# Windowed attention with a feed-forward layer: values of two pairs of heads in one block amid a first layer's products, with a new opening order and a last step that ends by token block

## Chip, cores and metric

The kernel runs on one core of one Trainium2 chip. The metric is the device time of one execution in microseconds (us): the median of 3 runs before is 913.11 us (913.05 to 916.48).

## The reference, cut to what matters

```python
B, H, S, D = 8, 8, 576, 64                     # q and k are multiplied by 8 when drawn
scores = (1 / np.sqrt(D)) * q @ k^T
mask_plain = (rel >= 0) & (rel < 32)           # heads 0 to 3; rel = query - key
mask_dil = (rel >= 0) & (rel < 128) & (rel % 4 == 0)    # heads 4 to 7
attn = softmax(where(mask, scores, -1e9))
x = (attn @ v).transpose(0, 2, 1, 3).reshape(4608, 512)
h = x @ w_in                                   # 512 x 2048
g = where(h >= 1, h, where(h <= -1, 0, (h + 1)**2 / 4))
return g @ w_out                               # 2048 x 512
```

(Shortened; the weights arrive as 64-bit floats.)

## The kernel before

**Attention.** The 64 heads are numbered n = 8 b + h and go in pairs (n even). Queries lie in six tiles of 96, each with its 128 keys. Heads 0 to 15 use plain fp32 matmuls and are part of the opening; for heads from 16 on (`native`), q and k are cast to a high part (`qs`, `kk` on ScalarE, L238 and L241) and a low part (`q_low` on VectorE, L245; `k_low` on GpSimd, L249). Scores come in pairs of tiles: `score_block(m, 0)`, `(m, 2)`, `(m, 4)`, two matmuls each (L332, bank `s`). VectorE masks (L356) and reduces (`lowest`, L284), ScalarE takes the exponential with its sum (`exp`, L382), GpSimd normalises (L419), VectorE transposes 32x32 blocks into `pt` (L430), and TensorE multiplies by the values (`weighted`, L532, bank `o`). The result is x, already transposed, cut in two: `x_high` copies into `xh` on ScalarE (L568), `x_low` subtracts into `xl` on VectorE (L573).

**Feed-forward.** The 4608 tokens are 9 blocks of 512 (`TOK`), each with 16 slices of 128 of the hidden dimension: 144 steps. `layer1(s, c)` for c = 0 to 3 makes 12 matmuls of 512 columns into one `h` bank (L598). Then a chain on two engines: `clamped` (VectorE, `y`, L608), `squared` (ScalarE, L611), `activated` (VectorE, into `h`, L614), `g_high` (ScalarE, `gh`, L621), `g_low` (VectorE, `gl`, L625), the last reader of the bank. `gh` and `gl` have two buffers each. `layer2(s - 2, m)` for m = 0 to 3 makes 12 matmuls from `gh` and `gl` into four `acc` banks (L637), two steps behind. The eight PSUM banks are two for `h`, two for `att` (scores, values), four for `acc`.

**What sets the order.** Steps up to 17 follow `OPENING`, a list of tokens written out by hand for all five engines: `S2.1` is the score of head 2, tile 1, `r` a reduction, `e` an exponential, `T` a transposition on TensorE with its copy `p`, `V` a value block with `x` and `l` behind it, `A` and `B` the two layers, `wi0` a load of weights, `W5` five spins. From step 18 on, TensorE's and SyncE's order is the program's, and ScalarE, VectorE and GpSimd get theirs from the scheduler. The loop at the end of the program runs layer 1 of step s, slot 2s, layer 2 of step s - 2, slot 2s + 1; `place(u, ...)` puts scores, transpositions and `values` of a pair into numbered slots, u = 27 + 4 (n - 16) onwards:

```python
place(u + 8, lambda n=n: transpose(n + 1))
place(u + 11, lambda n=n: values(n))
```

So a pair's two value blocks (`o{n}_0`, `o{n}_1`) stand together between a first layer and a second.

Of the kernel before, what the change touches and what calls it, by code (L numbers as in the profile page):

```python
# [31 lines left out]
DM, DF = 512, 2048  # L32
# [13 lines left out]
msk k0 q0 Q0 K0 q2 k2 q4 k4 S0.0 q6 S1.0 S0.1 S1.1 wi0 r0.0 r1.1 e0.0 k6 r1.0 r0.1 S0.2 e1.0 S1.2 v4 S0.3 S1.3  # L46
S0.4 e0.1 S1.4 S0.5 wi1 S1.5 e1.1 r0.2 r0.3 e0.2 r1.3 r1.5 k8 e0.3 r1.2 W2 S2.0 S3.0 r1.4 S2.1 e1.3 S3.1 r0.4
S2.2 S3.2 r0.5 e1.5 S2.3 v6 S3.3 S2.4 e1.2 r2.2 S3.4 S2.5 r3.2 S3.5 e1.4 r2.0 r2.3 wo1 e0.4 r3.0 r3.1 e0.5
r3.3 wo0 r3.4 e3.0 r2.1 i0 e3.3 r2.4 W5 S4.0 S5.0 r2.5 S4.1 e3.4 S5.1 i1 R0 S4.2 z2 R1 S5.2 r3.5 e3.1 S4.3 v0
S5.3 r4.1 e3.2 r5.0 r5.2 e3.5 v2 r4.3 S6.0 S7.0 awi0 r5.1 S6.1 n0 S7.1 r4.2 S6.2 S7.2 i3 r4.0 S6.3 e2 S7.3 k10  # L50
R3 r5.3 r7.3 r7.1 e5.1 r7.2 n3 e5.0 T0.0 r7.0 r6.3 e4.1 S4.4 wi2 S5.4 r6.1 S4.5 e4.0 S5.5 r6.0 r6.2 e4.2 u2
wi9 S6.4 n1 S7.4 e6.1 S6.5 S7.5 e6.3 r5.4 wi4 i2 e6.0 r6.4 R2 r4.4 e6.2 n2 r6.5 e4.3 p0.0 e6.5 q8 r5.5 r4.5
e6.4 r7.5 W8 T3.0 r7.4 e4.5 T1.0 i6 e4.4 R6 p3.0 T1.1 wi3 n6 T2.0 bwi0 p1.1 T3.1 i4 T0.1 p1.0 p2.0 wi6 e5.3
p3.1 V0.0 p0.1 R4 jwi0 e5.5 T6.0 e5.4 wo2 e7.1 n4 T6.1 hwi0 V0.1 x0.0.0 q10 e5.2 l0.0.0 awi1 T4.0 u5 T2.1
x0.1.0 V2.0 e7.5 e7.2 lwi0 p6.1 e7.3 p4.0 e7.4 x0.1.1 i5 l0.1.0 e7.0 p6.0 R5 u7 A0.0 n5 p2.1 x2.0.0 awi2
l0.1.1 T4.1 i7 l2.0.0 V2.1 awo0 R7 n7 T5.0 bwi1 T5.1 x2.1.0 wi14 p5.0 p4.1 T7.0 x2.1.1 wo4 bwo0 T7.1 p5.1 V4.0
l2.1.1 wi7 l2.1.0 bwi2 S8.0 wi5 jwi1 S9.0 S8.1 x4.0.1 x4.0.0 S9.1 V4.1 wi11 l4.0.1 p7.0 hwi1 v8 A0.1 l4.0.0
# [750 lines left out]
```

## Time and profile before

| what | us |
|---|---|
| median of 3 runs | 913.11 |
| lowest and highest | 913.05, 916.48 |
| profiled execution, own time | 912.37 |
| its span | 910.6 |
| TensorE busy | 898.5 (99%) |
| VectorE, ScalarE, GpSimd busy | 671.5, 492.8, 231.4 |

The span is shorter than the execution's own time by 1.8 us that lie outside of it. Busy time counts matmuls whose starts follow one another closely; their ends are modelled, so the distance between two starts is the better measure of what a matmul takes. A wait of an engine is listed with the operation that ended it.

### The profile page before, as it was taken

The numbers are of one execution on the slowest core, as the hardware profiler recorded it, in microseconds if no ns is written. First come the engines' busy times: TensorE is split into PE (matmuls) and PEld (weight loads), VectorE is DVE, ScalarE is ACT, GpSimd is POOL, SyncE is SP. The second block draws the span as 40 slices with busy tenths as digits, with TensorE's granted clock in tenths as the row PEclk, the third lists the DMA queues.
The fourth block names the chain that finished last, engine by engine and source line by source line (L and its number), as shares of the span: only waits on it lengthen the run. The fifth ranks groups of instructions, "written<-read, shape, count | busy, mean of one in ns | idle before, by whom it ended". The sixth has DMA issues, their size and how long they took to land.

```text
span 910.6 us, 14400 instructions
## 1 busy us (share of the span) xinstructions
PE 898.5 (99%) x4844; PEld 735.6 (81%) x4844; DVE 671.5 (74%) x1973; ACT 492.8 (54%) x1394; POOL 231.4 (25%) x155
## 2 busy tenths in 40 slices
PE   7999999999999999999999999999999999999998
PEld 6677887888888888888888888888888888888886
DVE  6988888888887888888888888888888643334333
ACT  7899966555555555556655555555555422223222
POOL 4546642322323222333222232322233000000000
PEclk9999999999999999999999999999999999999999
DMA  9953113122322123222312232212321010001001
GB/s 345 404 228 132 54 42 111 44 62 71 118 72 72 56 60 118 72 72 72 95 56 65 72 112 78 71 54 63 118 72 45 1 47 1 1 1 46 1 1 47
DMA packets 31178, 73.92 MB, mean 81 GB/s; under 512 B 3456, under 2 KB 4352, under 8 KB 31104
## 3 DMA queue, kind: packets, MB, share of 16 engines
q1 hardware_dynamic: 30816, 72.63, 24.4%
q8 instruction: 38, 0.62, 0.3%
q10 hardware_dynamic: 288, 0.38, 0.1%
q14 instruction: 36, 0.29, 0.1%
HBM read 63.55 MB, written 9.44 MB: 80 GB/s over the span
## 4 chain that ended last, share of the span: by engine, by line
PE 92%; ACT 3%; DMA 2%; DVE 2%; issue 0%; SPq 0%; ACTq 0%; DVEq 0%
PE acc L637 43%; PE h L598 41%; PE s L332 4%; PE o L532 3%; ACT c_place L382 1%; DMA kr<-k_in 1%; DMA wo_raw<-w_in 1%; PE s L317 1%; ACT c L382 0%; ACT xh L568 0%; ACT wi_raw L204 0%; DVE c L284 0%; PE t L462 0%; ACT wi_m L198 0%; DVE xl L573 0%
## 5 line engine op out<-in xcount | busy, mean ns | idle before, releaser
L637 PE MATMUL acc<-wo,gh 128*128 128x512 f32 x1152 | 384.0, 393 | 0.0
L598 PE MATMUL h<-xh,wi 128*128 128x512 f32 x1152 | 356.9, 391 | 0.2 <-DVE gl L625 0.2
L637 PEld LDWEIGHTS acc<-wo,gh 128*128 128x128 f32 x1152 | 216.5, 188 | 47.3
L598 PEld LDWEIGHTS h<-xh,wi 128*128 128x128 f32 x1152 | 209.3, 188 | 38.8 <-issue 0.4
L637 PE MATMUL acc<-wo,gl 128*128 128x512 f32 x576 | 225.2, 391 | 0.0
L598 PE MATMUL h<-xl,wi 128*128 128x512 f32 x576 | 224.4, 390 | 0.4 <-DVE xl L573 0.4
L249 POOL TENSOR_TENSOR kk<-kr,kk 128x608 fp32r<-128x608 f32 x48 | 93.6, 1949 | 404.7 <-ACT kk L241 395.4
L382 ACT ACTIVATE c<-c 96x128 f32<-96x128 f32 x330 | 128.9, 392 | 116.4 <-DVE c L284 116.1
L611 ACT ACTIVATE y<-y,consts 128x512 f32<-128x512 f32 x144 | 104.1, 723 | 123.4 <-DVE y L608 123.1
L621 ACT CAST gh<-h 128x512 fp32r<-128x512 f32 x144 | 84.3, 586 | 117.3 <-PE acc L637 115.8
L608 DVE TENSOR_SCALAR y<-h 128x512 f32<-128x512 f32 x144 | 99.2, 689 | 59.2 <-PE h L598 58.8
L614 DVE TENSOR_TENSOR h<-h,y 128x512 f32<-128x512 f32 x144 | 100.5, 698 | 49.2 <-ACT y L611 47.9
L598 PEld LDWEIGHTS h<-xl,wi 128*128 128x128 f32 x576 | 108.1, 188 | 24.0 <-DVE xl L573 0.9
L625 DVE TENSOR_TENSOR gl<-h,gh 128x512 fp32r<-128x512 f32 x144 | 98.7, 685 | 38.3 <-ACT gh L621 38.2
L637 PEld LDWEIGHTS acc<-wo,gl 128*128 128x128 f32 x576 | 108.1, 188 | 19.5
L430 DVE STREAM_TRANSPOSE pt<-c 32x192 f32<-32x192 f32 x288 | 106.0, 368 | 6.5 <-POOL c L419 3.1
L356 DVE TENSOR_TENSOR c<-s,fixed 96x256 f32<-96x256 f32 (+1 forms) x168 | 61.3, 377 | 34.8 <-PE s L332 33.8
L419 POOL TENSOR_TENSOR c<-c 96x768 f32<-96x768 f32 x52 | 76.3, 1467 | 24.1 <-DVE c L414 21.7
L284 DVE CUSTOM_DVE_ANT_0 c<-s,c 96x128 f32<-96x128 f32 x288 | 70.4, 280 | 1.0
L382 ACT ACTIVATION_READ_ACCUMULATOR c<-c 96x1 f32 x324 | 60.7, 187 | 0.0
L332 PEld LDWEIGHTS s<-kk,qs 128*96 128x96 f32 x288 | 46.2, 161 | 15.3
L332 PE MATMUL s<-kk,qs 128*96 128x256 f32 x288 | 57.3, 283 | 0.0
(80 smaller groups left out, 615.3 us busy)
## 6 DMA issues: line engine op xcount, KB each, us to landing
kr<-k_in SPq DMA_DIRECT2D x52, 304.0 KB, 3.3
qr<-q_in SPq DMA_DIRECT2D x52, 288.0 KB, 2.8
vt<-v_in SPq DMA_DIRECT2D x29, 384.0 KB, 4.0
out<-out SPq DMA_DIRECT2D x35, 256.0 KB, 2.5
wi_raw<-w_in SPq DMA_DIRECT2D x16, 512.0 KB, 7.7
wo_raw<-w_in SPq DMA_DIRECT2D x16, 512.0 KB, 8.8
v_place<-v_in SPq DMA_DIRECT2D x3, 384.0 KB, 7.5
k_place<-k_in SPq DMA_DIRECT2D x3, 304.0 KB, 5.8
```

The source lines that it names most:

```text
L249: nc.gpsimd.tensor_tensor(out=kk[:, 1], in0=kr, in1=kk[:, 0].bitcast(F32), op=ALU.subtract)
L332: PE.matmul(out=split_view(n, t0)[:, t - t0], lhsT=hd["qs"][:, t * QT : (t + 1) * QT], rhs=hd["ks"][:, :, t * QT : t * QT + 128], start=Tr ...
L382: nc.scalar.activation(out=c[:, t], in_=c[:, t], func=AF.Exp, bias=st[:, 0, t : t + 1], scale=-1.0, **total)
L419: engine.tensor_tensor(out=c, in0=c, in1=spread(factor(n)), op=ALU.mult)
L430: nc.vector.transpose(out=pts[n % 2][r : r + 32, :, 32 * g : 32 * g + 32], in_=heads[n]["c"][32 * g : 32 * g + 32, :, r : r + 32],)
L598: PE.matmul(out=hps[s], lhsT=ready[f"wi{f}"][:, w, 128 * c : 128 * c + 128], rhs=x[:, c], start=c == 0 and i == 0, stop=c == NC - 1 and i ...
L608: nc.vector.tensor_scalar(out=y, in0=hps[s], scalar1=-1.0, scalar2=1.0, op0=ALU.max, op1=ALU.min)
L611: nc.scalar.activation(out=ys[s], in_=ys[s], func=AF.Square, bias=half_t, scale=0.5)
L614: nc.vector.tensor_tensor(out=hps[s], in0=hps[s], in1=ys.pop(s), op=ALU.max)
L621: nc.scalar.copy(out=gs[s][0], in_=hps[s])
L625: nc.vector.tensor_tensor(out=gl, in0=hps.pop(s), in1=gh.bitcast(F32), op=ALU.subtract)
L637: PE.matmul(out=acc[m], lhsT=g[:, r], rhs=w[:, part], start=f == 0 and i == 0, stop=f == NF - 1 and i == 2,)
```

## The change

- `values` takes two pairs. For every second pair (n = 18, 22, ... 62) one block of 24 program matmuls stands after two of the four chunks of `layer1(s)`. Its first bank is the `h` bank of the step before, `h{(s + 1) % 2}`, and holds tiles 4 and 5 of the pair n; two `att` banks of 480 columns hold the rest. Of each bank all `xh` copies come first, then all `xl` subtractions.
- Half of the pairs' scores (n % 4 == 0) stand half a step later, some within a layer. Slots are counted in quarter steps.
- A second pair of `pt` buffers lies in `thirds`, the three buffers of 128 x 512 that the conversion of weights used, cleared by GpSimd at step 18. `xh`, `xl`, `h` have a tag per buffer; output rows are gathered in a former `xl` tile.
- `OPENING` is written anew; the masks come in two transfers, the first scores take three tiles instead of two, 18 instead of 13 weight tiles are cast on GpSimd (`cast_by_pool`), 6 instead of 8 heads are normalised on VectorE (`by_vector`), 16 instead of 21 copies of transposed blocks are VectorE's (`kept_by_vector`).
- The last two second layers go by token block. The last block's sum of step 142 is copied to SBUF by ScalarE, its last three products are made as two sets of 256 columns in `att` banks, added by VectorE and stored on two queues.

```diff
-OPENING = "... S6.3 e2 S7.3 k10 R3 r5.3 ... W8 T3.0 r7.4 e4.5 T1.0 i6 ..."
+OPENING = "... T1.0 v2 r4.4 e5.2 p3.0 T1.1 ... q8 W2 T3.1 e5.0 p0.1 T2.0 ..."
...
+    thirds = pool.tile([128, 3 * DM], U32, tag="m", name="thirds")
+    late_pts = thirds.bitcast(F32)[:, : 2 * NQ * QT].rearrange("p (n t j) -> p n t j", n=2, t=NQ)
...
-    first_tiles = 2
+    first_tiles = 3
...
-    def values(n):
-        for part in range(2):
-            weighted(n, part)
+    def values(n, s):
+        free = f"h{(s + 1) % 2}"
+        plan = (
+            (free, 1, ((n + 2, 4, 6),)),
+            ("att", 2, ((n, 0, 5),)),
+            ("att", 2, ((n + 2, 0, 4), (n, 5, 6))),
+        )
+        for tag, bufs, parts in plan:
+            op = ps.tile([128, 512], F32, tag=tag, name=f"o{n}_{parts[0][0]}_{parts[0][1]}", bufs=bufs)
...
             with tc.high_priority(offset=60):
-                for piece in range(len(pieces(n, part))):
-                    x_high(n, part, piece)
-                    x_low(n, part, piece)
+                lows = []
+                for pair, base, (lo, w, count, t, place) in pieces:
...
+                    nc.scalar.copy(out=xh, in_=src)
+                    lows.append((xl, src, xh))
+                for xl, src, xh in lows:
+                    nc.vector.tensor_tensor(out=xl, in0=src, in1=xh.bitcast(F32), op=ALU.subtract)
...
+    def last_block(o, gh, gl, w, rows):
+        nc.scalar.copy(out=o, in_=partial[0])
+        for i, queue in enumerate((nc.scalar, nc.sync)):
+            cols = slice(DM // 2 * i, DM // 2 * (i + 1))
+            rest = ps.tile([128, DM], F32, tag="att", name=f"rest{i}", bufs=2)[:, : DM // 2]
+            for k, (g, part) in enumerate(((gh, 0), (gl, 0), (gh, 1))):
+                PE.matmul(out=rest, lhsT=g, rhs=w[:, part, cols], start=k == 0, stop=k == 2)
+            nc.vector.tensor_tensor(out=o[:, cols], in0=rest, in1=o[:, cols], op=ALU.add)
+            queue.dma_start(out=rows[:, cols], in_=o[:, cols])
...
-        for j, at in ((0, u), (1, u + 4)):
-            place(at, lambda m=n + j: score_block(m, 0))
-            place(at + 1, lambda m=n + j: score_block(m, 2))
-            place(at + 2, lambda m=n + j: (score_block(m, 4), after(m)))
+        around = n % 4 == 0 and n > native
+        for j, ats in enumerate(((0, 0.75, 1.5), (4.5, 5.25, 6)) if around else ((0, 1, 2), (4, 5, 6))):
+            for t0, at in zip((0, 2, 4), ats):
+                place(u + at, lambda m=n + j, t0=t0: (score_block(m, t0), after(m) if t0 == 4 else None))
...
-        place(u + 11, lambda n=n: values(n))
+        if n % 4:
+            place(u + 10.5, lambda n=n, s=(u + 11) // 2: values(n - 2, s))
...
+    ends = {last + 1: [(last - 1, 0), (last - 1, 1)]}
+    ends[last + 2] = [(last, 0), (last - 1, 3), (last, 1), (last - 1, 2), (last, 2), (last, 3)]
```

How the values move, on TensorE. Before, the block of pair 32 stands between the first layer of step 51 and the second of step 49 (`h3_3` is token block 3, slice 3; `acc3_0` is block 3's first `acc`):

```order
L598 MATMUL h3_3_3906<-xh3_1957,wi3_642 128x512 x2
L598 MATMUL h3_3_3906<-xl3_1958,wi3_642 128x512
L532 MATMUL o32_0_3927<-pt0_66,vt32_3714 64x96
...
L532 MATMUL o32_1_3940<-pt0_66,vt32_3714 64x96
...
L637 MATMUL acc3_0_3865<-wo1_694,gh49_3797 128x512
L637 MATMUL acc3_0_3865<-wo1_694,gl49_3798 128x512
```

After, pairs 32 and 34 share one block, after six of the twelve matmuls of step 55 (`h3_7`). Its first rows, of the bank `o32_34_4`, are pair 34's tiles 4 and 5:

```order
L668 MATMUL h3_7_4098<-xh3_2126,wi7_988 128x512 x2
L668 MATMUL h3_7_4098<-xl3_2127,wi7_988 128x512
L628 MATMUL o32_34_4_4105<-thirds_68,vt34_3921 64x96 x4
L628 MATMUL o32_32_0_4114<-pt0_66,vt32_3679 64x96
...
L628 MATMUL o32_34_0_4129<-thirds_68,vt34_3921 64x96 x8
L628 MATMUL o32_34_0_4129<-pt0_66,vt32_3679 64x96
...
L668 MATMUL h3_7_4098<-xh3_2126,wi7_988 128x512 x2
L668 MATMUL h3_7_4098<-xl3_2127,wi7_988 128x512
...
L724 MATMUL acc3_0_3834<-wo5_1024,gh53_4004 128x512
```

The twelve pairs of matmuls of pair 32 left the place ahead of `acc`; the new block has `h` on both sides. A `x2` or `x8` counts equal rows in a run.

On ScalarE, the piece from one `y` to the next head's casts. Before, in step 58 (`y58`, `gh58`):

```order
L382 ACTIVATE c38_4323<-c38_4323 96x128 x2
L611 ACTIVATE y58_4343<-y58_4343,consts_65 128x512
L382 ACTIVATE c38_4323<-c38_4323 96x128 x2
L621 CAST gh58_4347<-h3_10_4330 128x512
L238 CAST qs39_4376<-qr39_4271 128x576
L241 CAST kk39_4377<-kr39_4273 128x608
```

After, in step 54, whose `gl` is the last reader of the bank that `o32_34_4` takes:

```order
L386 ACTIVATE c36_4026<-c36_4026 96x128 x3
L681 ACTIVATE y54_4053<-y54_4053,consts_65 128x512
L386 ACTIVATE c36_4026<-c36_4026 96x128
L242 CAST qs37_4073<-qr37_3974 128x576
L245 CAST kk37_4074<-kr37_3976 128x608
L691 CAST gh54_4057<-h3_6_4033 128x512
L386 ACTIVATE c36_4026<-c36_4026 96x128 x2
```

`gh` stood ahead of the casts `qs` and `kk`; it now stands behind them.

On VectorE, the same two pieces. Before, in step 58 (`s38_2` and `s38_4` are banks with scores of head 38, L356 masks, `ISA` is `lowest`):

```order
L608 TENSOR_SCALAR y58_4343<-h3_10_4330 128x512
L356 TENSOR_TENSOR c38_4323<-s38_2_4351,fixed_64 96x128 x2
L284 ISA c38_4323<-s38_2_4351,c38_4323 96x128
...
L614 TENSOR_TENSOR h3_10_4330<-h3_10_4330,y58_4343 128x512
L356 TENSOR_TENSOR c38_4323<-s38_4_4370,fixed_64 96x256
L625 TENSOR_TENSOR gl58_4348<-h3_10_4330,gh58_4347 128x512
L284 ISA c38_4323<-s38_4_4370,c38_4323 96x128
...
L245 TENSOR_TENSOR qs39_4376<-qr39_4271,qs39_4376 64x576
```

After, in step 54:

```order
L360 TENSOR_TENSOR c36_4026<-s36_2_4043,fixed_64 96x128 x2
L288 ISA c36_4026<-s36_2_4043,c36_4026 96x128
...
L678 TENSOR_SCALAR y54_4053<-h3_6_4033 128x512
L288 ISA c36_4026<-s36_2_4043,c36_4026 96x128
...
L360 TENSOR_TENSOR c36_4026<-s36_4_4067,fixed_64 96x256
L684 TENSOR_TENSOR h3_6_4033<-h3_6_4033,y54_4053 128x512
L288 ISA c36_4026<-s36_4_4067,c36_4026 96x128
...
L249 TENSOR_TENSOR qs37_4073<-qr37_3974,qs37_4073 64x576
L695 TENSOR_TENSOR gl54_4058<-h3_6_4033,gh54_4057 128x512
```

The masking of the second bank (`s36_2`) moved ahead of `y`, that of the third (`s36_4`) ahead of the activation into `h`, and the low part `qs37` ahead of `gl`.

## Rows read from the trace of the kernel before

**Rows 1.** The page's head, busy time and the granted clock of TensorE in 40 equal slices (tenths).

```profile
span 910.6 us, 14400 instructions
...
PE 898.5 (99%) x4844; PEld 735.6 (81%) x4844; DVE 671.5 (74%) x1973; ACT 492.8 (54%) x1394; POOL 231.4 (25%) x155
...
PEclk9999999999999999999999999999999999999999
```

**Rows 2.** The list of TensorE's waits, by line and operation and what ended them: us in total, times, longest.

```profile
PE s L317 <- DMA kr<-k_in: 1.4, 1, 1.4
PE t L462 <- POOL c L419: 1.2, 1, 1.2
PE o L532 <- DVE c L284: 1.2, 1, 1.2
...
PE h L598 <- DVE gl L625: 0.2, 1, 0.2
```

**Rows 3.** Busy time of each engine by stretch: the stretch, its length, then busy us and instructions of PE, PEld, DVE, ACT and POOL, the granted clock, the DMA share and GB/s.

```profile
160.00:400.00 240.00, 240.00 (x1274) 196.97 (x1273) 199.37 (x617) 135.23 (x407) 65.25 (x39) 1.00 0.25 73
400.00:600.00 200.00, 200.00 (x1068) 163.83 (x1066) 166.34 (x511) 114.27 (x344) 55.60 (x33) 1.00 0.26 76
```

**Rows 4.** TensorE's timeline, in two stretches: two of the single value matmuls of the opening, and one value block of the steady state between a first layer (`h`) and a second (`acc`). Columns: start, length, engine, line, operation, result and operands, shapes, count.

```profile
23.93 0.25 PE L532 MATMUL o<-pts_xh,v_place 128*64 128x96 f32 x1
...
24.10 0.25 PE L532 MATMUL o<-pts_xh,v_place 128*64 128x96 f32 x1
...
449.83 0.61 PE L598 MATMUL h<-xh,wi 128*128 128x512 f32 x2
...
451.64 0.39 PE L598 MATMUL h<-xl,wi 128*128 128x512 f32 x1
451.96 1.21 PE L532 MATMUL o<-pt,vt 128*64 128x96 f32 x24
453.10 0.50 PE L637 MATMUL acc<-wo,gh 128*128 128x512 f32 x1
453.44 0.40 PE L637 MATMUL acc<-wo,gl 128*128 128x512 f32 x1
...
455.77 0.39 PE L637 MATMUL acc<-wo,gh 128*128 128x512 f32 x1
```

**Rows 5.** TensorE's timeline over steps 58 and 59: the last matmul of `h58`, the first of two score pairs, the last `acc` (the second pair lies behind it) of the second layer, and the sixth matmul of the next first layer.

```profile
396.32 0.39 PE L598 MATMUL h<-xl,wi 128*128 128x512 f32 x1
396.55 0.40 PE L332 MATMUL s<-kk,qs 128*96 128x256 f32 x2
...
399.29 0.39 PE L637 MATMUL acc<-wo,gh 128*128 128x512 f32 x1
...
399.76 0.63 PE L598 MATMUL h<-xh,wi 128*128 128x512 f32 x2
...
400.91 0.39 PE L598 MATMUL h<-xl,wi 128*128 128x512 f32 x1
```

**Rows 6.** ScalarE's timeline there. In brackets, here and below: idle time just before, and what ended it.

```profile
399.72 0.59 ACT L621 CAST gh<-h 128x512 fp32r<-128x512 f32 x1 [0.37 <-PE acc L637]
400.20 0.68 ACT L238 CAST qs<-qr 128x576 fp32r<-128x576 f32 x1
400.78 0.70 ACT L241 CAST kk<-kr 128x608 fp32r<-128x608 f32 x1
```

**Rows 7.** VectorE's timeline there.

```profile
396.67 0.28 DVE L284 CUSTOM_DVE_ANT_0 c<-s,c 96x128 f32<-96x128 f32 x1
...
397.08 0.68 DVE L608 TENSOR_SCALAR y<-h 128x512 f32<-128x512 f32 x1
397.69 0.47 DVE L356 TENSOR_TENSOR c<-s,fixed 96x128 f32<-96x128 f32 x2
...
398.61 0.70 DVE L614 TENSOR_TENSOR h<-h,y 128x512 f32<-128x512 f32 x1
```

**Rows 8.** The timelines of VectorE and of TensorE at 156 us: the end of the reduction that frees a bank, and the value matmul that waited for it.

```profile
156.03 0.08 DVE L284 DVE_READ_ACCUMULATOR2_ANT c<- 96x1 f32 x1
...
156.25 0.72 PE L532 MATMUL o<-pt,vt 128*64 128x96 f32 x12 [1.21 <-DVE c L284]
```

**Rows 9.** TensorE's timeline in the opening: the first and the last of three groups of spins (matmuls on a constant) and the first transposition of head 7.

```profile
7.40 0.71 PE L269 MATMUL h<-consts 128*128 128x128 f32 x4
...
17.05 2.05 PE L269 MATMUL h<-consts 128*128 128x128 f32 x16
...
28.19 0.69 PE L462 MATMUL t<-fixed,c_place 96*128 96x96 f32 x6 [0.16 <-DVE c_place L419]
```

**Rows 10.** VectorE's normalisations in the first 30 us, as one line: count, shortest, median and longest ns, first and last start, form.

```profile
L419 DVE TENSOR_TENSOR c_place<-c_place,sums x2: 939/945/951, 22.1 to 27.1; 96x768 f32<-96x768 f32 x2
```

**Rows 11.** The timeline of all engines at the end, from the last matmul.

```profile
906.08 0.39 PE L637 MATMUL acc<-wo,gh 128*128 128x512 f32 x1
906.56 0.37 ACT L649 COPY out<-acc 128x256 f32<-128x256 f32 x1
...
906.96 0.42 DVE L650 COPY out<-acc 128x256 f32<-128x256 f32 x1 [1.12 <-ACT out L649]
907.41 0.33 SPq L652 DMA_DIRECT2D out<-out  x1
```

**Rows 12.** The page's list of loads and stores: result and source, queue, count, KB each, median us from issue to landing.

```profile
v_place<-v_in SPq DMA_DIRECT2D x3, 384.0 KB, 7.5
```

More of the change, by code (lines that the diff above doesn't have):

```diff
@@ L573, in x_low, with runs, place @@
         nc.vector.tensor_tensor(out=place(xl), in0=src, in1=place(xh).bitcast(F32), op=ALU.subtract)
-    def values(n):
-        for part in range(2):
-            weighted(n, part)
-            with tc.high_priority(offset=60):
-                for piece in range(len(pieces(n, part))):
-                    x_high(n, part, piece)
-                    x_low(n, part, piece)
+    def runs(n, first, last):
+        b, h = divmod(n, H)
+        tok0 = b * S
+        end = TOK - tok0 % TOK
+        a, z = first * QT, last * QT
+        if h < H // 2:
+            cuts = sorted({a, min(max(end, a), z), z})
+            for lo, hi in zip(cuts, cuts[1:]):
+                t, at = divmod(tok0 + lo, TOK)
+                yield lo - a, hi - lo, 1, t, lambda x, at=at, w=hi - lo: x[:, at : at + w]
+            return
+        spans = []
+        for r in range(a // CLS, (z - 1) // CLS + 1):
+            lo, hi = max(a - CLS * r, 0), min(z - CLS * r, CLS)
+            cuts = sorted({lo, min(max(end // DIL, lo), hi), hi})
+            for i, k in zip(cuts, cuts[1:]):
+                same = [p for p in spans if p[1:] == [r, i, k] and r - p[0] < 3]
+                if same:
+                    same[0][1] = r + 1
+                else:
+                    spans.append([r, r + 1, i, k])
+        for r0, r1, i, k in spans:
+            t, at = divmod(tok0 + DIL * i, TOK)
+            def place(x, r0=r0, r1=r1, at=at, w=DIL * (k - i)):
+                return x[:, at : at + w].rearrange("p (i r) -> p r i", r=DIL)[:, r0:r1]
+            yield CLS * r0 + i - a, k - i, r1 - r0, t, place
@@ L722, in body @@
     lag = 2
+    last = len(steps) - 1
+    ends = {last + 1: [(last - 1, 0), (last - 1, 1)]}
+    ends[last + 2] = [(last, 0), (last - 1, 3), (last, 1), (last - 1, 2), (last, 2), (last, 3)]
     with tc.manual_schedule(engines={engines.PE, engines.SP}):
-        for u in range(2 * start - 1):
+        for u in range(4 * (2 * start - 1)):
             slots.pop(u, None)
@@ L737, in body @@
             run(2 * s)
-            for m in range(TOK // 128):
-                layer2(s - lag, m)
+            for k, (i, m) in enumerate(ends.get(s, [(s - lag, m) for m in range(TOK // 128)])):
+                layer2(i, m)
+                if k < 3:
+                    run(2 * s + 0.25 + k / 4)
             run(2 * s + 1)
```

204 lines of the change are left out of this document (118 added, 86 removed).

## The prediction

> **What bounds the kernel now.** I read the page's head first: TensorE is busy for 99% of a span of 910.6 us, at nearly full granted clock [rows 1]. So the end moves only by what TensorE spends on something other than useful columns: switches between kinds of matmul, spins, waits, the opening and the tail. The list of its waits comes next [rows 2]: none is over 1.4 us, and the table by stretches shows TensorE busy for 240.00 of 240.00 us and 200.00 of 200.00 us of the steady state [rows 3]. The steady state has no wait to remove. It has slack behind it, though: VectorE is busy for 83% there and ScalarE for 56%, and a wait can be made. The timeline of TensorE around one block of values gives the price of a switch [rows 4]; the timelines of three engines over steps 58 and 59 the chain from one step's `h` to its `gl` [rows 5 to 7].
>
> **Merging the value blocks.** Twenty-four blocks of 12 program matmuls (24 recorded ones) become 12 blocks of twice that. Before, first-layer matmuls run at 1.81 us for eight, 0.226 each (449.83 to 451.64) [rows 4]. From the last of them at 451.64 to the twelfth `acc` at 455.77 are 4.13 us, where twelve at the plain pace take 2.72: a block costs 1.41 us. Its twelve pairs themselves go in every 0.083 us (23.93 to 24.10 is two of them), 1.00 us. The other 0.41 to 0.42 does not grow with pairs: entry 0.32 instead of 0.23, exit, a first `acc` to `acc` of 0.34 (453.10 to 453.44) and ten more at 0.233. Twelve switches fewer save 12 x 0.42 = **5.0 us**. The bounds: 2.8 if only entry and exit are saved (0.09 + 0.14 each), 5.0 if all is.
>
> By the Trainium skill, "TensorEngine Tiling (Array Packing)", Key Properties, a change of tiling mode drains the engine. This trace agrees in sign with its 0.09 and 0.14; that rule alone would give the 2.8, and says nothing of the slower `acc` behind the block, which the rows do show.
>
> **The wait that the merge makes.** The merged block stands amid the first layer of step s, and its first bank is the `h` bank of step s-1. So its first matmul needs `gl` of step s-1 finished, and TensorE stands still with everything behind it. Before, no value matmul touched an `h` bank. I walk the merge at s = 55 (pairs of heads 32 and 34) with durations of steps 58 and 59, which have the same work around them.
> - TensorE. Last matmul of `h58` at 396.32; six first-layer matmuls of the next step have started by 400.91, with two score pairs between [rows 5]. A score pair costs 0.47 - 0.23 = 0.24 us (399.29 to 399.76) wherever it stands, so scores half a step later cost TensorE nothing in themselves. After the change one pair lies inside the first layer (+0.24 to the `h`) and one between: arrival at 400.91 + 0.32 = 401.23.
> - VectorE. `lowest` of two tiles from 396.67 (0.41), `y` at 397.08 and `h` (activated) at 398.61 [rows 7]. The new order has a masking of two tiles (0.41) and one more `lowest` (0.21) ahead of `y`: `y` at 397.7 to 398.4, its square on ScalarE (0.72) to 399.2, activated from 399.2 to 399.9.
> - ScalarE. Before, `gh` ran at 399.72, as soon as the second layer had let go of its buffer, and the casts of the next head, `qs` (0.68) and `kk` (0.70), followed [rows 6]. The new order puts `qs37` and `kk37` **ahead of** `gh54`. They start 0.58 and 0.60 apart (400.20, 400.78, 401.38 in that row's pace): `qs` at 399.5, `kk` at 400.1, `gh` at 400.7 to 401.3.
> - `gl54` then runs 401.30 to 401.99. From VectorE's end to a released value matmul took 0.14 us (156.11 to 156.25) [rows 8]: 402.14. TensorE stands for 402.14 - 401.22 = **0.92 us**.
>
> Six merges have this order (heads 18, 26, ... 58). In five (22, 30, ... 54) one more exponential of 0.39 us stands ahead of the casts and partly lies in their way: I take 1.05. The last has no such casts in its way: 0.2. Together 6 x 0.92 + 5 x 1.05 + 0.2 = **11.0 us**. Lower bound 0.2 per merge, 2.4: even a `gh` that goes at once must wait for the second layer of step s-3 (last `acc` at 399.29 [rows 5]), so `gl` ends 0.2 late. Upper bound about 12, one `kk` cast (0.70) later in some. What is queued behind: on ScalarE the copies of values into `xh`, on VectorE those into `xl`, both after the block anyway, and the other half of the first layer of s on TensorE.
>
> Evictions, the second pair of `pt` buffers, high parts first, the memset: nothing. They lie on ScalarE, VectorE and GpSimd, which idle for 44, 17 and 73% there [rows 3]; without that cover the subtractions would delay `y` of step s, which has 12 matmuls of the second layer for its chain. Steady state: -5.0 + 11.0 = **+6.0** (from -2.6 to +9).
>
> **The opening.** The steps up to 18 do the same work in another order. Groups of spins (0.7 us from 7.40, 2.05 from 17.05 [rows 9]) and waits such as 1.4 for a load and 1.2 for a normalisation [rows 2] stand between the matmuls; the spins cover late data, and the change has 19 in its program for 15, so their number says nothing of the time. VectorE loses two normalisations of 0.945 us between 22 and 27 us [rows 10] and some copies; counted by order and row durations, 3.8 us less VectorE work stands ahead of `gl0`, and 4.5 less ahead of `gl1`. ScalarE's work to the exponentials of head 7 sums to 20.8 instead of 21.5. My walk puts the first transposition of head 7 at 27.4 instead of 28.19: -0.8. With VectorE that much ahead, the small waits on it behind that row, of which 0.2 for a `gl` [rows 2] is one, should go, and with them gaps in the first layers: -1.2 (0 to -3). The wait of 1.21 us at 156.25 belongs to a value block that no longer stands there: -1.4 with its small tail. More switches between values and first layer before 40 us: +0.35; spins that are not covered: +0.25. Sum **-2.8**, bounds -6 (the 4.0 of waits shown and 2.05 of the spins go) and +1.5 (values of head 2 late, below).
>
> **The end.** Before, the last `acc` starts at 906.08, ScalarE copies one half, VectorE waits for that copy and ends at 907.38, and the last store is issued at 907.41, 3.2 us before the span's end [rows 11]. After, the last block's earlier part is copied early, VectorE adds each half straight after its three matmuls of 256 columns, and the two halves leave on two queues: the last add ends near 907.0 (-0.4). The stores of the step before leave earlier, so the last should land in less than 3.2 us: -0.5. Sum **-0.9** (0 to -1.6).
>
> **Sum.** The profiled execution took 912.4 us, 0.7 under the median of 913.1. 912.4 + 6.0 - 2.8 - 0.9 = 914.7; on the median's footing **915.4 us**. A measurement of this kernel can tell about 0.5%, 4.6 us, from no change, so this counts as the same.
>
> **Rivals.**
> 1. *The chain keeps up.* If `gh` is not held by the casts, because `qs` and `kk` find their data and start while ScalarE would idle, the stall is 0.2 per merge: -5.0 + 2.4 - 2.8 - 0.9 = -6.3, **906.8 us**. For it: ScalarE is 56% busy, and idled 0.37 us before `gh` at 399.72 [rows 6]. Against it: `qs` must follow an exponential that waits for a masking that waits for a score, and these now come half a step later.
> 2. *The opening stands on a load.* Value matmuls of head 2 are now ahead of more first-layer work, and their values are asked for behind nineteen other loads. Such a load took 7.5 us to land [rows 12]. By bytes it lands near 22 us, and it decides from about 25 us on: every us after that is one us of TensorE. At 29 us the opening costs +1.5 instead of -2.8: **919.7 us**, slower. For it: the queues are full up to 40 us. Against it: TensorE's only wait for a load was one of 1.4 us [rows 2].
> 3. *Only the drains are saved.* If the slower `acc` after a block is a matter of how many pairs ran, merging saves 2.8 instead of 5.0: **917.6 us**. For it: the slowing lies behind the block and not at its edge. Against it: it lasts a dozen matmuls and is small.
>
> **How the numbers follow.** My forecast has 0.55, rival 1 0.25, rival 2 0.12, rival 3 0.08. Faster by over 0.5% (under 908.5): 0.20 of rival 1 and 0.02 of the forecast with its opening at the good bound, 0.22. Slower (over 917.7): 0.11 of rival 2, 0.04 of rival 3, 0.03 of the forecast, 0.18. The rest, 0.60, lies between. The range goes from 906.5, just under rival 1 (about 0.1 left out below), to 919.0, over rival 3 (about 0.07 above).
>
> **What would show it.** Right: twelve waits of TensorE for `gl`, at the first value matmul of each merge, of 0.9 to 1.1 us, and `gh` starting after the `kk` cast; 48 value matmuls in a row, then `h` matmuls that soon return to 0.226; no value wait at 156 us; the last add near 1.0 us after the last matmul starts. Wrong: waits at the merges of 0.2 or none (rival 1), a wait for `v_in` near 25 us (rival 2), or a saving per merge of 0.24 in TensorE's own times (rival 3).

## The result, and the profile after

The changed kernel takes **919.89 us** (median of 5 runs, 919.75 to 921.09) against 913.11 us (median of 5, 912.62 to 916.48): a ratio of 1.007 with a 95% interval of 1.0056 to 1.0085, slower by 6.8 us. The forecast was 915.4 (906.5 to 919.0).

The head of the page, answering to [rows 1]:

```profile
span 918.1 us, 14495 instructions
...
PE 895.1 (97%) x4855; PEld 737.5 (80%) x4855; DVE 669.6 (73%) x1982; ACT 493.0 (54%) x1402; POOL 234.4 (26%) x163
```

TensorE's busy time fell by 3.4 us and the span grew by 7.5. The list of its waits (us in total, times, longest), answering to [rows 2]:

```profile
PE o L628 <- DVE gl L695: 10.7, 11, 1.2
PE o L540 <- DVE pt L476: 1.6, 1, 1.6
PE h L668 <- DVE gl L695: 1.5, 2, 0.9
PE s L321 <- DMA qr<-q_in: 1.2, 1, 1.2
PE s L321 <- DMA k_place<-k_in: 1.1, 1, 1.1
```

Eleven waits for `gl` at the value blocks, 10.7 us, have joined the list; in the stretches of [rows 3] TensorE now idles:

```profile
160.00:400.00 240.00, 235.24 (x1277) 194.55 (x1276) 196.28 (x609) 133.52 (x403) 63.30 (x39) 1.00 0.25 74
400.00:600.00 200.00, 196.05 (x1058) 162.25 (x1057) 163.99 (x510) 112.32 (x341) 52.97 (x32) 1.00 0.26 76
```

One merge, at step 55, on TensorE, answering to [rows 4, 5]:

```profile
378.66 0.39 PE L668 MATMUL h<-xl,wi 128*128 128x512 f32 x1
380.13 0.55 PE L628 MATMUL o<-thirds,vt 128*64 128x96 f32 x8 [1.08 <-DVE gl L695]
...
382.26 0.73 PE L668 MATMUL h<-xh,wi 128*128 128x512 f32 x2
```

and on ScalarE and VectorE, answering to [rows 6, 7]:

```profile
377.62 0.66 ACT L242 CAST qs<-qr 128x576 fp32r<-128x576 f32 x1
378.18 0.69 ACT L245 CAST kk<-kr 128x608 fp32r<-128x608 f32 x1
378.78 0.57 ACT L691 CAST gh<-h 128x512 fp32r<-128x512 f32 x1
```

```profile
375.82 0.68 DVE L678 TENSOR_SCALAR y<-h 128x512 f32<-128x512 f32 x1
...
377.36 0.70 DVE L684 TENSOR_TENSOR h<-h,y 128x512 f32<-128x512 f32 x1 [0.31 <-ACT y L681]
...
378.49 0.76 DVE L249 TENSOR_TENSOR qs<-qr,qs 64x576 fp32r<-64x576 f32 x1
379.38 0.69 DVE L695 TENSOR_TENSOR gl<-h,gh 128x512 fp32r<-128x512 f32 x1
```

`qs` and `kk` run ahead of `gh` (378.78), `gl` ends at 380.07, and TensorE, which could have gone at 379.05, starts the block at 380.13. That is the wait that was forecast. `y` (375.82) was already late there: the layer's last matmul had ended at 374.7.

The second new entry, in the opening. TensorE, VectorE and GpSimd at 50 us (three fences):

```profile
51.65 0.40 PE L724 MATMUL acc<-wo,gh 128*128 128x512 f32 x1
53.64 1.21 PE L540 MATMUL o<-pt,vt 128*64 128x96 f32 x24 [1.59 <-DVE pt L476]
```

```profile
50.72 2.60 DVE L212 SCALAR_TENSOR_TENSOR thirds<-thirds,wo_raw 128x512 uint32<-128x512 uint32 x1
53.24 0.34 DVE L476 COPY pt<-t 128x192 f32<-128x192 f32 x1
...
57.03 2.93 DVE L423 TENSOR_TENSOR c<-c 96x768 f32<-96x768 f32 x1
```

```profile
49.67 1.85 POOL L392 TENSOR_TENSOR c<-c 96x768 f32<-96x768 f32 x1 [0.81 <-DVE c L288]
51.49 1.27 POOL L224 TENSOR_TENSOR wi<-thirds,wi 128x512 fp32r<-128x512 f32 x1
```

VectorE's joining of two words (L212) takes 2.60 us instead of 0.69. It ends 0.55 us after GpSimd's second instruction (52.76). The copy for which the value block waits stands behind it, and TensorE idles for 1.59 us. A second VectorE instruction, the normalisation of head 11, takes 2.93 us at 57.03, where 0.95 is usual.

**Where the 7.5 us of the span lie.** A mark that both kernels have is the last matmul of a first layer; the first mark below is the twelfth first-layer matmul. (In both opening tables `A1.0` and `A1.1` stand ahead of `A0.2` and `A0.3`, so this is the last of `A1.1` and not the end of step 0, as the expectations of runs 9 to 11 call it. It is the same matmul in both kernels.) In the trace of before, the first mark and the end of step 17:

```profile
35.14 0.39 PE L598 MATMUL h<-xl,wi 128*128 128x512 f32 x1
...
142.37 0.39 PE L598 MATMUL h<-xl,wi 128*128 128x512 f32 x1
```

and after:

```profile
34.67 0.40 PE L668 MATMUL h<-xl,wi 128*128 128x512 f32 x1
...
144.16 0.39 PE L668 MATMUL h<-xl,wi 128*128 128x512 f32 x1
```

| stretch, by the last matmul of a first layer | before | after | difference |
|---|---|---|---|
| start to the first mark | 35.14 | 34.67 | -0.5 |
| first mark to step 17 | 107.23 | 109.49 | +2.3 |
| step 17 to step 22 | 31.77 | 30.41 | -1.4 |
| step 22 to step 143 | 723.78 | 731.24 | +7.5 |
| step 143 to the span's end | 12.6 | 12.3 | -0.3 |

The rows sum to 7.6; the 7.5 is between rounded spans. A value block of 1.41 us that stood between steps 17 and 22 is now part of the first merge at step 23. Counted there, the merges cost +6.05 and the handover between the steps written out by hand and the rest +0.05.

The first two rows share one shift of work. Four score matmuls (`S8.2`, `S9.2`, `S8.3`, `S9.3`, recorded as eight) stood ahead of the first mark and now stand behind it. In the trace of before they take 0.61 us, up to the next row at 33.85:

```profile
33.24 0.68 PE L317 MATMUL s<-kr,qr 64*96 64x128 f32 x8
```

Without them the rows read +0.1 and +1.65. Nearly all of the 1.65 is waiting: between the two marks TensorE's waits of over 0.15 us sum to 0.63 us before and to 2.23 after, which are the 1.59 above and one of 0.64 for `gl` of step 0. Before and after:

```profile
40.58 0.88 PE L317 MATMUL s<-kr,qr 64*96 64x128 f32 x8 [0.40 <-DVE c L284]
41.70 0.69 PE L598 MATMUL h<-xh,wi 128*128 128x512 f32 x2 [0.23 <-DVE gl L625]
```

```profile
40.94 0.70 PE L668 MATMUL h<-xh,wi 128*128 128x512 f32 x2 [0.64 <-DVE gl L695]
```

### The profile page after: what moved, and what is told of

It reads as the page before. It is cut to its first block, busy times and chain, and to the rows that moved or that the text cites. A ratio compares the mean times of both kernels' runs of the same rounds, so it can differ in the third digit from the quotient of the medians.

```text
span 918.1 us, 14495 instructions
## 1 busy us (share of the span) xinstructions
PE 895.1 (97%) x4855; PEld 737.5 (80%) x4855; DVE 669.6 (73%) x1982; ACT 493.0 (54%) x1402; POOL 234.4 (26%) x163
## 4 chain that ended last, share of the span: by engine, by line
PE 62%; DVE 16%; ACT 10%; POOL 8%; issue 3%; DMA 1%; SPq 0%; ACTq 0%; DVEq 0%; POOLq 0%
PE acc L724 28%; PE h L668 28%; DVE thirds L434 4%; POOL kk L253 4%; POOL c L423 3%; ACT c L386 3%; DVE gl L695 3%; PE o L628 3%; ACT kk L245 2%; PE s L336 2%; ACT y L681 2%; ACT qs L242 2%; DVE pt L434 2%; DVE c L360 1%; DVE y L678 1%
## 5 line engine op out<-in xcount | busy, mean ns | idle before, releaser
L253 POOL TENSOR_TENSOR kk<-kr,kk 128x608 fp32r<-128x608 f32 x48 | 88.9, 1852 | 416.6 <-ACT kk L245 399.5
L434 DVE STREAM_TRANSPOSE thirds<-c 32x192 f32<-32x192 f32 x144 | 53.1, 369 | 8.5 <-POOL c L423 6.9
```

Source lines behind the costliest of these rows:

```text
L253: nc.gpsimd.tensor_tensor(out=kk[:, 1], in0=kr, in1=kk[:, 0].bitcast(F32), op=ALU.subtract)
L434: nc.vector.transpose(out=pt_of(n)[r : r + 32, :, 32 * g : 32 * g + 32], in_=heads[n]["c"][32 * g : 32 * g + 32, :, r : r + 32],)
```

## The experiments

All edits are made in the changed kernel, unless another is named; times beside 919.9 us. Ratios are against the kernel of before, with their 95% intervals.

**1. The h bank last in a merged block** (`bank_last`).

```diff
-            (free, 1, ((n + 2, 4, 6),)),
             ("att", 2, ((n, 0, 5),)),
             ("att", 2, ((n + 2, 0, 4), (n, 5, 6))),
+            (free, 1, ((n + 2, 4, 6),)),
```

> The changed kernel (919.9 us) with one edit: in each merged value block the h bank comes last of the three banks, not first. Theory A (the block's first matmul waits for gl of the step before, because its first bank is that step's h bank): twenty pairs of value matmuls, 20 x 0.083 = 1.7 us, now run ahead of the bank that needs gl, more than the wait of 0.9 to 1.2 us, so the eleven waits for gl (10.7 us in the trace) vanish or shrink under 0.2 us each: 909.5 us (908.5 to 911). The h bank is let go of later, which may add up to 0.2 us per merge ahead of the next first layer. Theory B (the block amid the layer is late for another reason, and the bank is only what the list names): waits of about the same sum stand at another bank, 918 to 920.

Measured: 914.9 us, ratio 1.0014 (1.0001 to 1.0026). TensorE's waits:

```profile
PE h L668 <- DVE xl L651: 4.2, 5, 1.0
```

All waits for `gl` at the blocks are gone, so theory A's cause holds. Its price (909.5) did not: five of the twelve merges have a new wait of 0.4 to 1.0 us, of the next first layer. VectorE and TensorE at the merge of step 31:

```profile
231.52 1.14 DVE L651 TENSOR_TENSOR xl<-o,xh 128x288 fp32r<-128x288 f32 x3 [0.82 <-ACT xh L648]
232.56 1.89 DVE L434 STREAM_TRANSPOSE pt<-c 32x192 f32<-32x192 f32 x5
234.46 1.63 DVE L651 TENSOR_TENSOR xl<-o,xh 128x288 fp32r<-128x288 f32 x6
```

```profile
235.46 0.39 PE L724 MATMUL acc<-wo,gh 128*128 128x512 f32 x1
236.23 0.70 PE L668 MATMUL h<-xh,wi 128*128 128x512 f32 x2 [0.39 <-DVE xl L651]
```

Five transpositions (1.89 us) stand between the subtractions of the block; the last of these frees the h bank at 236.09, and the next first layer waits.

**2. Value blocks per pair, as before** (`pair_blocks`).

```diff
-        if n % 4:
-            place(u + 10.5, lambda n=n, s=(u + 11) // 2: values(n - 2, s))
+        place(u + 11, lambda n=n: values_pair(n))
```

(`values_pair` is the `values` of before.)

> The changed kernel with its values per pair again, between first and second layer, as before the change; scores half a step later, opening, end and buffers as changed. Theory A (the steady state loses 10.7 us of waits for gl and gains about 5.0 of switches; opening, handover and end together cost some 1 us): 914.0 us (913 to 915). Theory B (the loss stands in the opening, and the waits for gl take the place of other lost time): 917 or more.

Measured: 914.84 us, ratio 1.0017 (1.0006 to 1.0027). Theory A: merging alone costs about 5 us, and all the rest of the change 1.3 us over the 913.58 of before's runs beside it. Of that rest 0.7 us stands in the steady state: steps 22 to 143 take 724.47 us here, 723.78 before.

**3. The cast of k on GpSimd** (`k_cast_gpsimd`).

```diff
-        nc.scalar.copy(out=split_tiles(n)[1][:, 0], in_=heads[n]["kr"])
+        copy = nc.gpsimd.tensor_copy if n > 17 and n % 4 == 1 else nc.scalar.copy
+        copy(out=split_tiles(n)[1][:, 0], in_=heads[n]["kr"])
```

> The changed kernel with one edit: for heads 21, 25, ... (n % 4 == 1) the cast kk runs on GpSimd, so that ScalarE's gh of the step before a merge no longer has it ahead. Theory A (gh is late by the casts qs and kk): gh comes 0.6 us earlier, the waits fall from 0.9-1.2 to 0.3-0.6 us, 11 x 0.6 = 6.6 us less: 913.3 us (912 to 915). Theory B (gh is held by the second layer that has yet to let go of its buffer, not by the casts): no change, 919.9. Theory C (the low part of q on VectorE is held while GpSimd works, and stands ahead of gl): waits as long as now or longer, 919.9 or more.

Measured: 921.92 us, ratio 1.0092 (1.0074 to 1.011). Theory A is wrong as it stood. At step 55, on ScalarE and on VectorE:

```profile
379.27 0.66 ACT L242 CAST qs<-qr 128x576 fp32r<-128x576 f32 x1
379.83 0.57 ACT L692 CAST gh<-h 128x512 fp32r<-128x512 f32 x1
```

```profile
379.01 0.70 DVE L685 TENSOR_TENSOR h<-h,y 128x512 f32<-128x512 f32 x1 [0.31 <-ACT y L682]
...
380.14 0.76 DVE L250 TENSOR_TENSOR qs<-qr,qs 64x576 fp32r<-64x576 f32 x1
380.93 0.69 DVE L696 TENSOR_TENSOR gl<-h,gh 128x512 fp32r<-128x512 f32 x1
```

`gh` runs straight behind `qs` now and ends at 380.40. But `gl` stands in VectorE's order behind two `lowest` and the low part of q, and starts at 380.93, when that is done. TensorE waits 1.23 us, against 1.08, and 11.9 us over all merges, against 10.7. The time is in theory C's range, but the low part took its usual 0.76 us, so theory C's hold by GpSimd is not the cause. In the changed kernel the low part ends at 379.25 and `gh` at 379.35: two queues are late by nearly the same amount, and shortening one shows the other.

**4. The copy ahead of the joining** (`copy_first`).

```diff
-... T9.0 jwo2 g2 ... V8.0 p9.1 d2 ...
+... T9.0 g2 ... V8.0 p9.1 jwo2 d2 ...
```

> The changed kernel with one token of the opening moved: VectorE's joining of wo2 (2.60 us at 50.72, where such an instruction takes 0.69 elsewhere) goes behind the copy p9.1 that the value block of pair 8 waits for. Theory A (that wait, 1.59 us at 53.64, is the copy's place behind the joining, and nothing else is late there): the wait goes, 918.4 us (918.0 to 918.8). Theory B (the time is lost anyway a few steps on, because VectorE is as late as before): 919.5 to 920. In either case the joining still takes over 1 us if it is GpSimd's running instruction that holds it.

Measured: 920.0 us, ratio 1.0072 (1.0054 to 1.009). The wait of 1.59 us is gone, and from the first mark step 4 ends 1.6 us sooner. Two steps on stand two new ones:

```profile
65.29 0.72 PE L540 MATMUL o<-pt,vt 128*64 128x96 f32 x12 [0.59 <-ACT pt L476]
66.61 0.72 PE L540 MATMUL o<-pt,vt 128*64 128x96 f32 x12 [0.60 <-ACT pt L476]
```

From the first mark to step 17 it takes 109.24 us instead of 109.49: theory B.

**5. The opening of before** (`old_opening`): `OPENING`, `first_tiles`, `cast_by_pool`, `whole_pass`, `sum_apart`, `by_vector` and `kept_by_vector` as they were; the identity still in a load of its own.

```diff
-    first_tiles = 3
+    first_tiles = 2
...
-    whole_pass = (2, 11)
-    sum_apart = (5, 9, 14, 15)
-    by_vector = (8, 11, 12, 13, 14, 15)
+    whole_pass = (2, 12)
+    sum_apart = (5, 7, 14)
+    by_vector = (4, 7, 8, 9, 11, 12, 14, 15)
```

> The changed kernel with the opening table of before, and with the tables that belong to it (first tiles, casts on GpSimd, heads on VectorE); steady state and end as changed. Theory A (the new opening itself costs time: 1.8 us up to step 17, and 0.9 us of a wait for gl at 154 us, where VectorE transposes head 17 ahead of it): 917.2 us (916.5 to 918). Theory B (the openings are alike, and the difference up to step 17 is of the loads in this one execution): 919 to 920.5.

Measured: 920.06 us, ratio 1.007 (1.0045 to 1.0095). By the time, neither theory is shown: the four runs lie between 919.0 and 921.2, and 917.2 was not reached. The profile tells more. The order does set the distance: from the first mark to step 17 it takes 107.30 us again. But the first mark stands at 35.95 in this execution, 1.3 us later, and ahead of the first merge VectorE is later: a score pair waits 0.46 us for it, and the block 1.48 where it had waited 0.99. So 0.7 us of the 2.2 is left in the profiled span (917.5 against 918.1).

**6. The h bank in the middle** (`bank_middle`).

```diff
-            (free, 1, ((n + 2, 4, 6),)),
             ("att", 2, ((n, 0, 5),)),
+            (free, 1, ((n + 2, 4, 6),)),
             ("att", 2, ((n + 2, 0, 4), (n, 5, 6))),
```

> The changed kernel with the h bank as the second of a merged block's three banks, instead of the first (or the last, where VectorE subtracted from it only behind transpositions, and the next first layer waited 4.2 us in all). Theory A (what counts is only when gl is needed and when the h bank is free again): ten pairs, 0.83 us, run ahead of the h bank; waits for gl of 0.1 us in six merges and 0.3 in five, 2 us in all, none for the h bank's subtraction: 911.3 us (910 to 912.5). Theory B (any place of that bank costs about 4 us, at one end or the other): 914 to 916.

Measured: 911.5 us, ratio 0.9983 (0.9971 to 0.9995), theory A. The waits for `gl` at the blocks:

```profile
PE o L628 <- DVE gl L695: 1.4, 5, 0.3
```

No wait for the bank's subtraction is left. The remaining 1.4 us stand in five of the six merges of heads 18, 26, ... 58.

**7. Head 17's transpositions behind `gl`** (`bank_middle_t17`), on top of 6.

```diff
-... n17 j17 g17 d17
+... n17 j17 g17 d17 t17.0.0 t17.0.1 t17.1.0 t17.1.1 t17.2.0 t17.2.1
...
-        place(u + 8, lambda n=n: transpose(n + 1))
+        if n > native:
+            place(u + 8, lambda n=n: transpose(n + 1))
```

> As bank_middle, and the transpositions of head 17 stand behind gl of step 17 in VectorE's order, written into the opening. Theory A (VectorE's 2.3 us of transpositions ahead of gl make the wait of 0.9 us of the first layer of step 19): 0.9 us less than bank_middle, 910.4. Theory B (gl is late there for y and masking too): the wait goes half at most, or comes back a step later, within 0.4 us of bank_middle.

Measured: 911.83 us, ratio 0.9978 (0.9965 to 0.9991). Step 19 ends 1.19 us earlier relative to step 17, and by step 23 1.03 us of it are lost again: a score pair waits 0.31 and the first merge 0.50, where in `bank_middle` neither waits. Theory B.

**8. Old opening and h bank in the middle** (`old_opening_bank_middle`): the edits of 5 and 6 together.

> Both: the opening of before, and the h bank in the middle of a merged block. If the two losses add up (theory A of both): 911.3 - 2.7 = 908.6 us (907.5 to 910), under before's 913.1 by 4.5, of which some 5.0 are switches saved, 2 waits left and 0.5 the end. If the waits of the steady state stand whatever the bank: 912 or more.

Measured: **910.64 us**, ratio 0.9967 (0.9955 to 0.9979), the lowest median of all versions and lower than both kernels, though the intervals of runs 6 to 10 overlap. It is not the 908.6 of the sum: from the first mark to step 17 it takes 107.26 us, but the mark stands at 35.93 (34.43 in the profile of `bank_middle`), and a score pair and the first merge wait 0.45 and 0.53 us.

**9. VectorE freed in the opening** (`vector_freed`), on top of 6.

```diff
-... T9.0 jwo2 g2 ... V8.0 p9.1 d2 ...
+... T9.0 g2 ... V8.0 p9.1 d2 jwo2 ...
-    by_vector = (8, 11, 12, 13, 14, 15)
+    by_vector = (8, 12, 13, 14, 15)
```

> bank_middle (911.5 us) with two edits of the opening that keep VectorE from standing behind GpSimd: the joining of wo2 (2.60 us) goes behind the copy p9.1 and gl of step 2, and the normalisation of head 11 (2.93 us, 0.95 elsewhere) goes to GpSimd. Theory A (these two, 3.9 us over their usual length, make steps 0 to 17 take 109.4 us from the end of the first to that of the last first layer, where the opening of before takes 107.3): 107.3 to 108.4 us there, neither instruction over 1.7 us, and 910.0 us in all (909.4 to 910.9). Theory B (ScalarE, busy for 9.4 to 9.8 of 10 us in most of that stretch, is the bound, and whatever is gained comes back at a later wait, as with copy_first): over 109 us there, 911 to 912.

Measured: 911.16 us, ratio 0.9974 (0.9964 to 0.9985). From the first mark to step 17 it takes 108.39 us instead of 109.43, as theory A has it: about half of the 2.2 us goes with these two instructions moved. TensorE's waits there are now 0.64 for `gl` and 0.60 for a copy. Another joining is held, 1.73 us at 60.04. The time of the whole kernel lies in theory B's range, and 0.3 us against `bank_middle` can't be told from none.

**10. One load for masks and identity** (`old_opening_one_mask`), on top of 8.

```diff
-            nc.scalar.dma_start(out=fixed[:QT, : 3 * 128], in_=fixed_in[:, : 3 * 128])
-            nc.sync.dma_start(out=ident, in_=fixed_in[:, 3 * 128 :])
+            nc.scalar.dma_start(out=fixed[:QT], in_=fixed_in)
```

> old_opening_bank_middle (910.6 us) with the masks and the identity in one load on ScalarE's queue, as before the change, and none on SyncE's. Theory A (the extra load ahead on SyncE's queue makes the first layer of step 0 end at 35.9 instead of 35.1 us): 909.8 us. Theory B (the 0.8 us are the scatter of the loads from one execution to the next): 910.6.

Measured: 910.88 us, ratio 0.9979 (0.9967 to 0.9991). The first mark stands at 35.11 in the profiled execution, not 35.93, yet the median is no lower. Inconclusive.

**11. Before, once more** (`before_again`), with no edit.

> The kernel of before, once more, to see how much the opening scatters between executions: the end of the first layer of step 0 stood at 35.14 us, that of step 17 at 142.37. If the scatter is in the loads alone, the first moves by up to 1 us and the distance of the two, 107.2, by less than 0.2.

Measured, in one execution: 912.7 us, the first mark at 35.55, from there to step 17 107.29. Over all profiles of this study the first mark stands between 34.3 and 35.95 (with the new opening alone between 34.3 and 35.6), so the -0.5 of one pair of profiles is within the scatter. The distance from there to step 17 is 107.2 to 107.3 in five executions with the old opening, 109.4 to 109.5 in six with the new one unedited.

**12. VectorE beside GpSimd** (`vector_and_gpsimd`). In place of the kernel's body, for each stretch:

```python
nc.vector.tensor_tensor(out=D[i], in0=D[i], in1=one, op=ALU.mult)
nc.gpsimd.tensor_tensor(out=G[i], in0=G[i], in1=one, op=ALU.mult)
```

seven times each, or with the kinds that the expectation names.

> Not the kernel: only eight VectorE and eight GpSimd instructions at a time on tiles of 128x512, in five stretches that begin together; nothing of the reference is computed. VectorE takes two operands from SBUF, or one, or one from PSUM and one from SBUF, beside GpSimd products of two operands, and two from SBUF beside GpSimd copies. Theory A (a VectorE instruction with two fp32 operands in SBUF waits until GpSimd's running instruction is over, and the other way about): beside products, the first kind takes turns, each instruction as long as the other engine's and its own together (about 2 us); the other two kinds take 0.6 to 0.7 us as without GpSimd. Theory B (both share bandwidth): all kinds get slower by a like share.

Measured, VectorE's timeline of the middle three stretches and of the last (a row with x7 is seven instructions in that time):

```profile
16.91 0.69 DVE L114 TENSOR_TENSOR d<-d,g 128x512 f32<-128x512 f32 x1
17.63 11.64 DVE L116 TENSOR_TENSOR d<-d,one 128x512 f32<-128x512 f32 x7
...
31.15 9.77 DVE L120 TENSOR_SCALAR d<-d 128x512 f32<-128x512 f32 x7
...
42.80 5.04 DVE L124 TENSOR_TENSOR d<-bank,one 128x512 f32<-128x512 f32 x7
...
54.03 7.72 DVE L116 TENSOR_TENSOR d<-d,one 128x512 f32<-128x512 f32 x7
```

Beside GpSimd's products, two SBUF operands take 1.66 us each (11.64 / 7) where a first one takes 0.69, one operand 1.40 (9.77 / 7), and an operand in PSUM 0.72 (5.04 / 7). In the last stretch the first of the seven still runs beside a product and takes 1.63; the six beside copies follow one another every 1.01 us. Beside two operands GpSimd's products come every 1.67 us too, so each engine has one turn per 1.67 us; beside the PSUM stretch they come every 1.34. Theory A holds in kind for two operands and for PSUM. Its size, about 2 us, does not: 0.69 and 1.34 would sum to 2.03, so some 0.4 us of the two overlap. That one SBUF operand is held too was not expected; no stretch shows that kind without GpSimd.

## Why the prediction was wrong

By the profiles +2.3 us were forecast and +7.6 came: +0.05 of the difference is in the merging, +4.6 in the opening, +0.6 in the end.

**Merging and its wait, +6.0: right in kind, and in size with some luck.** Measured +6.05. The waits came at the bank that the walk named: 10.7 us in eleven waits against 11.0 in twelve. By kind the sizes were crossed. The six of the kind of step 55 took 0.99 to 1.19 us, where 0.92 was worked out, and the five of the kind of step 31 took 0.81 to 0.83, where 1.05 was taken for one more exponential. The errors of +1.1 and -1.2 us cancel, and that is luck. `bank_last` and `bank_middle` show that the bank is their cause.

The switches: between `pair_blocks` and `bank_middle` lie 914.84 - 911.5 = 3.3 us, with 1.4 us of waits left, so 4.7 us saved, where the working took 5.0. Counted in the profiles from step 22 to step 143, the changed kernel and `bank_middle` against before and `pair_blocks` give 4.0 to 5.4, so rival 3 and its 2.8 are out. This goes beyond what the prediction took from the Trainium skill's "TensorEngine Tiling (Array Packing)", Key Properties, the drain alone. That the moved scores cost TensorE nothing was not borne out: `pair_blocks`, which has them, is 0.7 us slower than before in steps 22 to 143 with no wait over 0.15 us. Which of its edits does that was not tried.

One link of the walk was told as the cause and isn't alone: `gh` behind the casts. `k_cast_gpsimd` took the longer cast away and gained nothing, since VectorE's own queue (masking, `lowest`, the low part of q) brings `gl` at the same time. The walk's VectorE part ended with the activated `h`; the two `lowest` and the low part behind it were not in its sum. They end 0.1 us before `gh` (379.25 and 379.35), so leaving them out did no harm here.

**The opening, -2.8: this step failed.** Measured: -0.5 to the first mark, +2.3 to step 17, +0.05 at the handover, +1.8 in all, 4.6 us off. By its terms:
- *First transposition of head 7 at 27.4 instead of 28.19 (-0.8).* It came at 28.11. TensorE waited 1.15 and 1.05 us for first loads (1.41 and 0.37 before), and its spins after the first group took 5.4 us instead of 4.1, where +0.25 had been put for spins. Up to the first mark waits and these spins together came to 10.8 us, against 10.1.
- *Waits on VectorE go (-1.2).* This is the main error. Up to the first mark TensorE's waits on VectorE did fall, from 3.2 to 2.1 us, but loads and spins took that up; behind it they grew by 1.6 us. VectorE did have 4.0 us less work ahead of `gl0` (29.3 us busy against 33.3), as counted, but `gl0` started only 0.75 us earlier (40.12 against 40.87). VectorE stood idle for the rest, 10.9 us against 7.6: 8.5 us until a matmul of TensorE was done (6.2 before), 1.35 until a copy `xh` of ScalarE was (0.5 before). In the end `gl0` stood behind five reductions in VectorE's own order, with `gh0` done 0.2 us before. The wait for `gl0`, which the prediction named as one that goes, grew from 0.23 to 0.64 us. Less work on an engine that waits for others gave back little.
- The other part of that error lies behind `gl0`. Total work up to `gl17` is the same (125.0 us busy, 124.7 before); the change moves VectorE's work from before the first mark to after it. There, two of its instructions take 1.9 and 2.0 us over their usual length while GpSimd works, and the wait of 1.59 us stands behind one of them. Rows of before showed the like. The first 160 us have eleven VectorE instructions over 0.25 us longer than usual, the longest 1.81 us at 83.75 where 0.95 is usual, and all end 0.54 to 0.82 us after an instruction of GpSimd. After the change there are seven such, ending as long after one of GpSimd's, and only the two at 50.72 and 57.03 let two of GpSimd's go first (none before). The prediction priced every VectorE instruction of the opening by its usual length. With these two moved, `vector_freed` gets back 1.04 of the 2.2 us; with the first alone behind its copy, `copy_first` gets back 0.25.
- *The wait at 156 us goes (-1.4).* It went, and one of 0.90 for `gl` of step 17 came in its place, as VectorE transposes head 17 first, and nothing was gained (+0.05):

```profile
151.31 2.27 DVE L434 STREAM_TRANSPOSE pt<-c 32x192 f32<-32x192 f32 x6
153.61 0.69 DVE L695 TENSOR_TENSOR gl<-h,gh 128x512 fp32r<-128x512 f32 x1
```

and on TensorE:

```profile
154.36 0.73 PE L668 MATMUL h<-xh,wi 128*128 128x512 f32 x2 [0.90 <-DVE gl L695]
```

`bank_middle_t17` removed that wait, and most of it came back by the first merge. This points to VectorE's work up to step 23 as what sets the time there, not the order of two of its instructions.

By the Trainium skill, "SBUF — State Buffer", section "SBUF: two separate sides", VectorE and GpSimd share a pair of ports as an exclusive lock, held for a whole instruction, against VectorE instructions with two SBUF inputs or in a mode that uses both ports. The held instruction at 50.72 agrees (two SBUF inputs, an end 0.55 us after GpSimd's), and so does run 12 in kind: two SBUF operands are held, one with an operand in PSUM is not. Its 1.67 us are less than the 2.03 of two whole instructions one behind the other. Whether its one-operand stretch ran in such a mode no row shows. The prediction should have drawn on it. That the 18 casts on GpSimd instead of 13 make the holds longer is not shown: no run changed them alone.

**The end, -0.9: a third.** Measured -0.3. The last store is issued 9.2 us after the last first layer instead of 9.5, and lands 3.1 us later in both kernels, where half a us was to be won. Both adds run at the very end, since the first waits for its three products, which stand directly ahead of the second three:

```profile
914.22 0.28 PE L706 MATMUL rest<-wo,gh 128*128 128x256 f32 x1
914.25 0.76 DVE L707 TENSOR_TENSOR out<-rest,out 128x256 f32<-128x256 f32 x2 [1.09 <-PE rest L706]
...
915.03 0.33 SPq L708 DMA_DIRECT2D out<-out  x1
```

**Rivals.** Rival 1 (`gh` in time) did not happen. Rival 2 had the sign and nearly the time (919.7), but not the place: no value block waited for `v_in`; what was late was VectorE. Its price was the bound +1.5 for the opening, and +1.8 came; that the two are close is chance. What stays open: the opening's order was not tried with `gl0` ahead of the five reductions, nor with fewer casts on GpSimd, and what sets the place of the first mark (34.3 to 35.95 us) is not known.

## What to carry to other kernels

A bank borrowed from another stage ties two chains together at both ends: look for when its last reader is done and for when its next writer comes, and put it where both have slack; here the middle of the block was worth 8.4 us over the front. Take work from the engine that the chain of waits names: here 4.0 us less VectorE work ahead of `gl0` brought it forward by 0.75 us, and VectorE stood idle for the rest. A wait removed by order alone came back a few steps on in both runs that tried it (4 and 7). Price VectorE instructions with SBUF operands by the rows in which GpSimd runs beside them, not by their usual length.

## What was not expected of the hardware

VectorE and GpSimd take turns, instruction by instruction, on operands in SBUF: in run 12 1.66 us instead of 0.69 for a product of two on 128x512 while GpSimd makes products too (1.01 beside its copies), 1.40 for an operation with one SBUF operand, 0.72 (next to nothing) with one operand in PSUM. A VectorE instruction can lose twice running: at 50.72 it let two GpSimd instructions pass and took 2.60 us, at 57.03 again (2.93 instead of 0.95). In other rows VectorE went ahead of GpSimd's next instruction (before, at 68.95: 1.07 us); what decides is not known.
